# One-query attention over 65,536 keys: second K tile in halves, K1 transposes ahead of the V weights, a tail of 24 slots, and unused matmuls

## The chip, the cores and the metric

The kernel runs on one core of one Trainium2 chip. The metric is the device time of one execution in microseconds (us); lower is better. Each execution is given a state, fast or slow, by its time and the clock that it was granted. PE is the matrix engine (TensorE), PEld its weight loads, DVE the vector engine, ACT the scalar engine, SP the engine that issues nearly all loads.

## The reference

```python
B, Hq, Hkv, Sq, Sk, D = 1, 32, 8, 1, 65536, 128      # bf16
k = jnp.repeat(k, 4, axis=1); v = jnp.repeat(v, 4, axis=1)
scores = jnp.einsum("bhqd,bhkd->bhqk", q, k) * D ** -0.5
return jnp.einsum("bhqk,bhkd->bhqd", _softmax(scores), v)
```

There is one query for each of 32 heads, and 8 groups of keys and values. K and V together are 268.44 MB and are used once. The output is tiny.

## The kernel before

K and V of one group g are cut into two tiles each, K(g,0), K(g,1), V(g,0), V(g,1): 128 partitions x 256 rows x 128 values of bf16, 8.39 MB. The kernel keeps three tiles on chip: one slot for V, one for K(.,0), one for K(.,1). Each load waits until the tile that held its slot has been used.

The loads, in the order in which SP issues them (all code in this section is shortened, with comments added). `s_sc` counts groups of score matmuls; `s_vc` counts half V tiles that PE has finished, two for a tile.

```python
def load_k(g, b):
    SP.wait((s_sc, 16 * g - 8 + 8 * b if g else 0))       # the K tile before it in this slot is used
    cuts = k_cuts.get((g, b), [0, SL])                    # k_cuts: K(0,0) in halves, K(7,1) in quarters
    ...
def load_v(g, b):
    done = 2 * (2 * g + b)
    if (g, b) == (G - 1, 1):                              # the last V tile: a half when half the slot is free, then CUTS
        ...
    elif (g, b) in ((G - 2, 1), (G - 1, 0)):              # V(6,1), V(7,0): in halves, as the slot comes free
        for i in range(2):
            SP.wait((s_vc, done - 1 + i))
            load(v, g, b, 0, s_v[i], 128 * i, 128 * i + 128)
    ...
    else:
        SP.wait((s_vc, done))                             # the whole V tile before it is used
        load(v, g, b, 0, s_v[0])
load_k(0, 0); load_k(0, 1)
for g in range(1, G):
    for b in range(2):
        load_k(g, b); load_v(g - 1, b)
load_v(G - 1, 0); load_v(G - 1, 1)
```

DVE transposes each K tile in four parts in place. It also transposes the softmax weights of a V tile into `et`, which PE needs for that V tile:

```python
for g in range(G):
    for _ in transposes(g, 0): pass                       # 4 x 128x4096
    if g:
        DV.wait((s_vc, 4 * g - 2))                        # PE has finished V(g-1,0): et may be overwritten
        weights(g - 1, 1)
    for i, _ in enumerate(transposes(g, 1)):
        if i == 1: bank_max(g, 0); bank_max(g, 1)
    bank_max(g, 2); ...; softmax(g); ...; weights(g, 0); ...
```

PE runs one loop: scores of K(h,j), then the V tile two behind. Matmuls on V are 64 a tile, each covering 4 row slots; the last `TAIL` slots of the last tile are multiplied one by one in another accumulator after the loop, so that DVE can gather the large accumulator meanwhile:

```python
for ch in range(4):                       # quarters of the V tile
    ...                                   # waits for the loads
    for tt in range(16 if ch < 3 else 12): i = wide(ch, tt)
    if ch == 1: i.then_inc(s_vc, 1)       # half of the V slot is free
```

## Time and profile before

The kernel before takes 636.14 us (median of 4 runs, 635.71 to 636.58).

| | before |
|---|---|
| span of the profile | 634.2 us |
| load queue q1: busy share of 16 DMA engines | 98.4% |
| busy share of PE, DVE | 55%, 55% |
| queue dry near 100 us / near 587 us | 1.50 / 1.93 us |
| end of last load packet to end of span | 5.49 us |

These are lines of the page of the kernel before: the DMA engines' busy tenths and GB/s in 40 slices of the span, the load queue (packets, MB, share), and two DVE groups (busy time, mean ns | idle time before them, and what ended it).

```profile
DMA  8999999999999999999999999999999999999896
GB/s 364 455 438 434 426 397 397 446 413 459 401 459 401 463 401 459 438 422 455 405 459 401 459 403 459 434 422 459 405 455 409 455 409 451 406 438 417 372 429 262
...
q1 hardware_dynamic: 6200, 268.44, 98.4%
...
L237 DVE STREAM_TRANSPOSE io<-io 128x4096 uint32<-128x4096 uint32 x64 | 279.5, 4414 | 92.2 <-DMA io<-in_k_dram 92.2
...
L281 DVE STREAM_TRANSPOSE et<-ex 128x512 bf16<-128x512 bf16 x32 | 21.0, 691 | 97.8 <-PE vacc L359 95.9
```

Loads are busy almost throughout, so only a moment in which the queue is dry, and the time after the last byte, can be saved. Two slices stand out: the 372 GB/s slice near the end, and the last one. DVE waits 97.8 us in all just before it transposes weights, almost all of it for PE's V matmuls; yet most of that waiting costs nothing.

The packet records behind the page give each load packet's start and duration. At each moment one can count how many of the 16 engines have a packet in flight, n, and add up (16-n)/16: that is the "dry" time above. In the steady stretch the last byte of a tile comes 19.34 us after that of the one before: 8.39 MB / 19.34 us = 434 GB/s. The Trainium skill ("DMA: Bandwidth & Descriptors", Specifications) gives 435 GB/s as the ceiling of the fabric, and this trace agrees.

The first hole is seen from the load issues (timeline of SP: start, duration, engine, line, op):

```profile
67.25 0.33 SPq L125 DMA_DIRECT2D io<-in_k_dram  x1
100.68 0.33 SPq L125 DMA_DIRECT2D io<-in_v_dram  x1
```

The issue at 67.25 is K(1,1). The issue at 100.68 is V(0,1). It waits for PE to finish V(0,0). By then the tile issued before it, K(1,1), has landed, so nothing is left in the queue. The second hole is seen in the windows view (window, length, busy time and count of PE, PEld, DVE, ACT, POOL, then granted PE clock, DMA share, GB/s; a packet is booked where it starts), and its cause in the timeline of the last group:

```profile
core 0: us, PE busy (x) PEld busy (x) DVE busy (x) ACT busy (x) POOL busy (x), PEclk, DMA share, GB/s
584.00:586.00 2.00, 2.00 (x16) 0.85 (x19) 0.25 (x1) 0.00 (x0) 0.00 (x0) 1.00 1.07 459
586.00:588.00 2.00, 1.60 (x32) 0.54 (x23) 0.59 (x2) 0.00 (x0) 0.00 (x0) 1.00 0.19 82
588.00:590.00 2.00, 0.91 (x20) 0.50 (x24) 0.00 (x0) 0.00 (x0) 0.00 (x0) 1.00 0.86 262
```

```profile
559.45 1.30 DVE L281 STREAM_TRANSPOSE et<-ex 128x512 bf16<-128x512 bf16 x2 [11.32 <-PE vacc L359]
560.68 8.73 DVE L237 STREAM_TRANSPOSE io<-io 128x4096 uint32<-128x4096 uint32 x2
...
570.51 8.75 DVE L237 STREAM_TRANSPOSE io<-io 128x4096 uint32<-128x4096 uint32 x2
...
585.70 1.90 PE L359 MATMUL vacc<-io,et 128*16 128x512 bf16 x32
...
587.64 27.70 SPq L125 DMA_DIRECT2D io<-in_v_dram  x8
```

Between 586 and 588 us only 82 GB/s start. DVE sat idle for 11.32 us until PE had finished V(6,0), only then transposed the weights and then the four parts of K(7,1), whose first two parts had landed by then (this tile lands between 549.5 and 569.1 us). PE did K(7,1) before V(6,1), so it got to the middle of V(6,1) at 587.6, and V(7,0) could be issued only at 587.64.

The end of the kernel before: 16 single slots (L425), the gather (L355), the scaling (L307); the store follows.

```profile
629.03 1.87 PE L425 MATMUL pf<-io,et 128*4 128x128 bf16 x16 [0.47 <-issue]
...
630.70 0.63 PE L355 MATMUL pf<-vs,sel 128*4 128x128 f32 x2
631.43 0.34 DVE L307 TENSOR_SCALAR o<-pf,rl 4x128 bf16<-4x128 f32 x1 [1.30 <-PE pf L355]
```

### The profile page before, as it was taken

The numbers are of one execution on the slowest core, as the hardware profiler recorded it, in microseconds if no ns is written. First come the engines' busy times: TensorE is split into PE (matmuls) and PEld (weight loads), VectorE is DVE, ScalarE is ACT, GpSimd is POOL, SyncE is SP. The second block draws the span as 40 slices with busy tenths as digits, with TensorE's granted clock in tenths as the row PEclk, the third lists the DMA queues.
The fourth block names the chain that finished last, engine by engine and source line by source line (L and its number), as shares of the span: only waits on it lengthen the run. The fifth ranks groups of instructions, "written<-read, shape, count | busy, mean of one in ns | idle before, by whom it ended". The sixth has DMA issues, their size and how long they took to land. (4 is left out here: it accounts for less than half of the span.)

```text
span 634.2 us, 7031 instructions
## 1 busy us (share of the span) xinstructions
PE 349.6 (55%) x2122; PEld 139.5 (22%) x2122; DVE 347.5 (55%) x239; ACT 36.7 (6%) x72; POOL 7.3 (1%) x39
## 2 busy tenths in 40 slices
PE   0738385836628365382744818447183572858425
PEld 0213132312203122130311303113031230323102
DVE  4938666639156490654807457084660936576201
ACT  0000200020000200002000020000200002000100
POOL 1000000000000000000000000000000000000000
PEclk9978798966959779596896968969587695979755
DMA  8999999999999999999999999999999999999896
GB/s 364 455 438 434 426 397 397 446 413 459 401 459 401 463 401 459 438 422 455 405 459 401 459 403 459 434 422 459 405 455 409 455 409 451 406 438 417 372 429 262
DMA packets 6309, 268.50 MB, mean 423 GB/s; under 512 B 800, under 2 KB 800, under 8 KB 1184
## 3 DMA queue, kind: packets, MB, share of 16 engines
q1 hardware_dynamic: 6200, 268.44, 98.4%
q10 hardware_dynamic: 104, 0.02, 0.0%
q14 instruction: 4, 0.03, 0.0%
q8 instruction: 1, 0.02, 0.0%
HBM read 268.44 MB, written 0.01 MB: 423 GB/s over the span
## 5 line engine op out<-in xcount | busy, mean ns | idle before, releaser
L383 PE MATMUL sc<-io,wz 128*128 x1024 | 272.0, 417 | 211.8 <-PEq L345 169.1
L237 DVE STREAM_TRANSPOSE io<-io 128x4096 uint32<-128x4096 uint32 x64 | 279.5, 4414 | 92.2 <-DMA io<-in_k_dram 92.2
L383 PEld LDWEIGHTS sc<-io,wz 128*128 x1024 | 105.9, 103 | 374.9 <-issue 296.6
L359 PE MATMUL vacc<-io,et 128*16 128x512 bf16 x1020 | 65.3, 409 | 20.1 <-PEq L345 20.1
L281 DVE STREAM_TRANSPOSE et<-ex 128x512 bf16<-128x512 bf16 x32 | 21.0, 691 | 97.8 <-PE vacc L359 95.9
L262 ACT ACTIVATE ex<-sc,nmb 128x512 bf16<-128x512 f32 x32 | 21.5, 685 | 556.9 <-DVE nmb L259 556.9
L242 DVE TENSOR_REDUCE mx<-sc 128x1 f32<-128x512 f32 x32 | 20.7, 667 | 47.6 <-PE sc L383 47.6
L359 PEld LDWEIGHTS vacc<-io,et 128*16 128x16 bf16 x1020 | 26.6, 93 | 57.8 <-issue 36.7
L355 PE MATMUL pf<-vs,sel 128*4 128x128 f32 x20 | 5.2, 358 | 26.8 <-PEq L345 26.8
L251 DVE TENSOR_REDUCE m<-pt 1x4 f32<-1x128 f32 x8 | 2.2, 279 | 22.5 <-PE pt L413 22.5
L272 ACT ACTIVATE sc<-zero 128x2048 f32<-128x2048 f32 x7 | 13.2, 1880 | 0.3
L224 POOL COPY wz<-qT 32x16 bf16<-32x16 bf16 x32 | 6.1, 190 | 509.8 <-PE sc L383 504.5
L372 PE MATMUL pb<-ls,sel 128*4 128x4 f32 x18 | 1.8, 169 | 15.7 <-PEq L345 15.7
L290 DVE TENSOR_SCALAR vs<-vacc,sely 128x128 f32<-128x128 f32 x8 | 2.6, 323 | 14.0 <-PE vacc L359 14.0
L293 DVE SCALAR_TENSOR_TENSOR vs<-vacc,sely,vs 128x128 f32<-128x128 f32 x24 | 8.4, 350 | 0.8
L355 PEld LDWEIGHTS pf<-vs,sel 128*4 128x4 f32 x20 | 1.3, 87 | 27.2 <-issue 27.2
L262 ACT ACTIVATION_READ_ACCUMULATOR ex<-sc,nmb 128x1 f32 x32 | 6.5, 202 | 0.0
L415 PE MATMUL pb<-one,nrow 1*128 1x1 f32 x16 | 2.8, 241 | 5.7 <-PEq L345 5.7
L372 PEld LDWEIGHTS pb<-ls,sel 128*4 128x4 f32 x18 | 1.2, 88 | 18.9 <-issue 18.7
L300 DVE MEMSET vacc<- 128x512 f32 x7 | 3.4, 485 | 1.3 <-DVE vs L293 1.3
L415 PEld LDWEIGHTS pb<-one,nrow 1*128 1x128 f32 x16 | 2.3, 183 | 7.0 <-issue 7.0
L259 DVE COPY nmb<-pb 128x1 f32<-128x1 f32 x8 | 1.3, 157 | 4.3 <-PE pb L415 4.3
(27 smaller groups left out, 21.3 us busy)
## 6 DMA issues: line engine op xcount, KB each, us to landing
io<-in_v_dram SPq DMA_DIRECT2D x5, 4096.0 KB, 18.3
io<-in_k_dram SPq DMA_DIRECT2D x2, 4096.0 KB, 16.6
io<-in_k_dram SPq DMA_DIRECT2D x4, 2048.0 KB, 40.3
io<-in_v_dram SPq DMA_DIRECT2D x1, 2048.0 KB, 10.9
io<-in_v_dram SPq DMA_DIRECT2D x1, 1024.0 KB, 13.0
io<-in_v_dram SPq DMA_DIRECT2D x1, 512.0 KB, 13.9
io<-in_v_dram SPq DMA_DIRECT2D x2, 256.0 KB, 14.1
io<-in_k_dram SPq DMA_DIRECT2D x14, 48.1
```

The lines of the kernel that those rows point to most:

```text
L224: gp.tensor_copy(out=wz[r, :, c0:c0 + H].rearrange("p (s w) h -> p s w h", s=2), in_=qTb[r, :, :, g, :],).then_inc(s_w, 1)
L237: dve.transpose(out=part.bitcast(u32), in_=part.bitcast(u32)).then_inc(s_kt, 2)
L242: return DV.mark(dve.tensor_reduce(out=mx[:, b:b + 1], in_=sc[:, 512 * b:512 * b + 512], axis=AX.X, op=ALU.max))
L262: a = act.activation(out=ex[:, b, :], in_=sc[:, 512 * b:512 * b + 512], func=ACT.Exp, bias=nmb[:, :], scale=SCALE, accum_out=ls[:, b:b + 1],)
L272: ACTQ.mark(act.activation(out=sc[:, :], in_=zero[:, 0:1].to_broadcast([P, 4 * 512]), func=ACT.Copy))
L281: dve.transpose(out=et[:, i, :], in_=ex[:, 2 * b + i, :]).then_inc(s_et, 1)
L293: i = dve.scalar_tensor_tensor(out=vs[:, :], in0=vacc[:, y, :], scalar=sely[:, y:y + 1], in1=vs[:, :], op0=ALU.mult, op1=ALU.add,)
L300: n = DV.mark(dve.memset(vacc[:, :, :], 0.0))
L355: return pe.matmul(out=fin, lhsT=sel[:, :], rhs=vs[:, :], skip_group_check=True, **kw)
L359: return pe.matmul(out=vacc[32 * c:32 * c + 16, :, :], lhsT=et[:, ch // 2, w0:w0 + 16], rhs=io[:, PS * ch + 4 * tt:PS * ch + 4 * tt + 4, : ...
L383: i = pe.matmul(out=bass.AP(sc, r_o, [[2048, P], [1, 512]]), lhsT=bass.AP(wz, r_w + ((2 * s + e) * WB - 4 * u), [[4 * WB, P], [1, P]]), rh ...
L415: pe.matmul(out=pb[:, 0:1], lhsT=nrow[:, :, :].rearrange("o x h -> o (x h)"), rhs=one[:, :], start=True, stop=True,).then_inc(s_pe, 1)
```

## The change

The intent: let the second K tile be transposed as it arrives, let DVE use its wait before the V weights for half of K1, end the large V accumulator sooner (24 single slots for 16, with finer last cuts), and keep the matrix engine's clock up with unused matmuls in each V tile's middle.

```diff
-TAIL = 16
-CUTS = [0, 128, 192, 224, 240, 248, 256]
+TAIL = 24
+CUTS = [0, 128, 192, 224, 232, 240, 248, 256]
...
-    k_cuts = {(0, 0): [0, 128, 256], (G - 1, 1): [0, 64, 128, 192, 256]}
+    k_cuts = {(0, 0): [0, 128, 256], (0, 1): [0, 128, 256], (G - 1, 1): [0, 64, 128, 192, 256]}
...
-        if g:
-            DV.wait((s_vc, 4 * g - 2))
-            weights(g - 1, 1)
         for i, _ in enumerate(transposes(g, 1)):
             if i == 1:
+                if g:
+                    DV.wait((s_vc, 4 * g - 2))
+                    weights(g - 1, 1)
                 bank_max(g, 0)
                 bank_max(g, 1)
...
                     if ch == 1:
                         i.then_inc(s_vc, 1)
+                        for _ in range(3):
+                            pe.matmul(
+                                out=pt[0:16, :], lhsT=et[:, 0, 0:16], rhs=et[:, 0, :],
+                                start=True, stop=True,
+                            )
...      (the tail's loop bounds and waits follow from TAIL and CUTS)
```

More of the change, by code (lines that the diff above doesn't have):

```diff
@@ L399 @@
                         take(s_v[max(ch - 1, 0)], 16)
-                    for tt in range(16 if ch < 3 else 12):
+                    for tt in range(16 if ch < 3 else (SL - TAIL) % PS // 4):
                         if (ch, tt) == (3, 8):
@@ L405 @@
                         i.then_inc(s_vc, 1)
+                        for _ in range(3):
[3 more added lines that the diff above has]
+                            )
                 i.then_inc(s_vb, 1)
                 with pe.If(h * 2 + j < 2 * G + 1):
-                    for tt in range(12, 16):
+                    for tt in range((SL - TAIL) % PS // 4, 16):
                         i = wide(3, tt)
@@ L422 @@
         if x % 8 == 0:
-            pe.wait_ge(s_v[len(CUTS) - 3 + x // 8], 16)
-        w0 = (12 + x // 4) * 32 + 16 + 4 * (x % 4)
+            pe.wait_ge(s_v[4 + x // 8], 16)
+        w0 = t % PS // 4 * 32 + 16 + 4 * (x % 4)
         pe.matmul(
```

## The prediction

> **What bounds the kernel.** The load queue. The page's DMA table gives it 98.4% of the 16 engines' span, 268.44 MB at 423 GB/s; PE and DVE are busy 55% each. In the DMA packet records the 32 K/V tiles land 19.34 us apart in the steady stretch. The Trainium skill ("DMA: Bandwidth & Descriptors", Specifications) gives a ceiling of 435 GB/s; the trace agrees (434). So only dry time of the queue and the work after the last byte can be saved.
>
> **Where it is dry** (packet records over 16 engines: 3.3 us in all):
> - About 100-102 us, 1.5 us. Load V(0,1) waits for the last matmul of V(0,0); it is issued at 100.68, when K(1,1) has just landed. The first packets after it take 3.3 instead of 2.42 us, and this tile lands 22.3 us after the one before: about 2.5-2.9 us lost.
> - About 586.5-589 us, 1.9 us (window 586-588: 82 GB/s). The first half of V(7,0) waits for the middle of V(6,1), which PE reaches at 585.7 because it does K(7,1) first; that waited for DVE, which sat 11.3 us (timeline) behind the weights of V(6,1) while K(7,1) was landing. About 2-2.5 us lost with the restart.
>
> **The change, costed.**
> 1. K(0,1) in halves: DVE waited 10.6 us for the whole tile until 42.1. With a half at about 32.5 PE bounds (8 groups at 2.5 us): K(0,1) ends near 58 instead of 66 us, softmax(0) 8 us sooner, V(0,0) done at about 93-95 instead of 100.7. Hole 1 closes. Cost: 32 KB packets run at 425.5 against 431.6 GB/s, +0.28 us for the tile.
> 2. Half of K1 before the V weights: two 4.40 us transposes move into DVE's idle time; the weights come about 4 us later, off the path. K(7,1) ends on PE at about 581 instead of 585.7, V(7,0) is issued near 583, before the queue is dry at 586.5. Hole 2 closes, with only some 2 us to spare. Steady groups have 8-10 us of queue slack: nothing.
> 3. Tail 24: at the half clock (0.5 from 594 to 631) one single V slot takes 0.117 us. vacc and collect end about 1 us sooner, but PE, with three groups of 8 at 0.94 us, ends near 630.9 as before. About 0.
> 4. Unused matmuls: 3 x 0.43 us cold or 0.22 warm, 16 tiles, all in slack. The skill ("TensorE: Matmul & The Clock Gate", Part 1) says a busy window of about 3.4 us releases the clock; a cold half tile is 3.59 us and becomes 4.9, so the clock may be full at the end. Then the last group of 8 is 0.5 us shorter. Chance even: -0.3 us.
>
> **Sum.** -2.6 - 2.3 + 0.3 - 0.3 = -4.9; rounded for holes that don't close fully: 636.56 to 632.0 us (-0.7%). Range 630.3 to 634.0. Faster by over 2%: 0.01; within: 0.98; slower: 0.01.
>
> **What would show it.** Tiles land 19.4 us apart near 101 and near 588; V(0,1) issued at 92-96 us; no 11 us DVE idle before the V weights in the last group; PE's K(7,1) ends by 582; queue share over 98.8%. Steady groups: same 38.7 us period. The clock in the last 10 us tells of step 4.
>
> **What would make it wrong.** Hole 2 closing only half (2 us of slack); engines drifting apart, so that a removed hole returns as an uneven finish; the unused matmuls delaying the V half; a cold 24-slot tail costing 0.3-0.5 us.

## The result, and the profile after

The changed kernel takes 631.3 us (median of 4 runs, 630.88 to 632.21) against 636.14. The ratio is 0.9926, 95% interval 0.9909 to 0.9943. A ratio here is of the fast runs of both kernels; it is not quite the ratio of the medians quoted, and in the later jobs not exactly that of the means of all runs either. Ten more runs of the unedited kernel in two later jobs gave medians of 631.89 and 632.24, so the first median is on the lucky side (the second job ran on another chip than the third); by the medians of the three jobs the changed kernel is 3.8 to 4.8 us faster than the one before.

The same lines of the page after:

```profile
DMA  8999999999999999999999999999999999999996
GB/s 367 433 459 408 458 408 455 412 454 412 454 412 454 417 450 417 450 417 450 421 446 421 446 425 442 425 442 425 446 425 442 429 437 429 409 433 431 431 428 247
...
q1 hardware_dynamic: 6488, 268.44, 98.9%
...
L237 DVE STREAM_TRANSPOSE io<-io 128x4096 uint32<-128x4096 uint32 x64 | 279.8, 4417 | 162.8 <-DMA io<-in_k_dram 162.8
...
L281 DVE STREAM_TRANSPOSE et<-ex 128x512 bf16<-128x512 bf16 x32 | 20.6, 683 | 15.4 <-PE vacc L359 13.5
```

The queue's share is 98.9%, the slice at 372 GB/s is gone, and DVE now waits 15.4 instead of 97.8 us before weights; it waits for loads instead (162.8 us). Both holes are closed: V(0,1) is issued at 93.86 us, and the windows of the second hole are full.

```profile
59.85 0.33 SPq L125 DMA_DIRECT2D io<-in_k_dram  x1
93.86 0.33 SPq L125 DMA_DIRECT2D io<-in_v_dram  x1
```

```profile
584.00:586.00 2.00, 0.00 (x0) 0.00 (x0) 0.00 (x0) 0.00 (x0) 0.00 (x0) 0.72 0.95 410
586.00:588.00 2.00, 1.67 (x17) 0.60 (x21) 0.00 (x0) 0.00 (x0) 0.00 (x0) 0.50 0.95 410
588.00:590.00 2.00, 2.00 (x21) 0.53 (x13) 0.00 (x0) 0.00 (x0) 0.00 (x0) 0.50 1.14 492
```

The last group after: the first two parts of K(7,1) are transposed as they land, the weights follow without idle time before them, and PE begins V(6,1) at 578.65 instead of 585.70.

```profile
552.17 4.45 DVE L237 STREAM_TRANSPOSE io<-io 128x4096 uint32<-128x4096 uint32 x1 [6.83 <-DMA io<-in_k_dram]
...
557.08 4.45 DVE L237 STREAM_TRANSPOSE io<-io 128x4096 uint32<-128x4096 uint32 x1 [0.47 <-DMA io<-in_k_dram]
...
561.45 1.26 DVE L281 STREAM_TRANSPOSE et<-ex 128x512 bf16<-128x512 bf16 x2
...
563.81 8.75 DVE L237 STREAM_TRANSPOSE io<-io 128x4096 uint32<-128x4096 uint32 x2
...
578.65 1.90 PE L359 MATMUL vacc<-io,et 128*16 128x512 bf16 x32
```

At the end the clock was granted in full in this profile, and 24 slots took less time than 16 before:

```profile
618.87 0.89 PE L408 MATMUL pt<-et 128*16 128x512 bf16 x3
...
624.66 1.50 PE L431 MATMUL pf<-io,et 128*4 128x128 bf16 x24 [0.65 <-DMA io<-in_v_dram]
...
626.00 0.38 PE L355 MATMUL pf<-vs,sel 128*4 128x128 f32 x2
626.48 0.34 DVE L307 TENSOR_SCALAR o<-pf,rl 4x128 bf16<-4x128 f32 x1 [0.91 <-PE pf L355]
```

But the last load packet ends only 3.88 us sooner (624.87 against 628.75), although 3.4 us of dry time and the slow restarts after it are gone. The windows view of the last microseconds of loading shows where some of it went. Before, the loads run at nearly the full rate until the last packet ends at 628.75:

```profile
624.00:626.00 2.00, 1.88 (x16) 0.45 (x16) 0.00 (x0) 0.00 (x0) 0.00 (x0) 0.50 0.97 406
626.00:628.00 2.00, 1.07 (x12) 0.21 (x12) 0.00 (x0) 0.00 (x0) 0.00 (x0) 0.50 1.01 387
```

After, the rate falls off more than 2 us before the last packet ends at 624.87:

```profile
620.00:622.00 2.00, 1.04 (x16) 0.35 (x16) 0.00 (x0) 0.00 (x0) 0.00 (x0) 1.00 1.00 382
622.00:624.00 2.00, 0.98 (x10) 0.26 (x10) 0.00 (x0) 0.00 (x0) 0.00 (x0) 1.00 0.58 216
```

In the last 6 us before the last packet's end, the engines were idle for 0.30 us before and 1.62 us after (packet records). So the mean engine finished 628.75-0.30 = 628.45 us before and 624.87-1.62 = 623.25 us after, 5.2 us sooner, and the slowest one only 3.9 us. About 1.3 us of the gain came back as an uneven finish.

### The profile page after: what moved, and what is told of

It is laid out like the page before. It is cut to its first block, busy times and chain, and to the rows that moved or that the text cites. A ratio compares the mean times of both kernels' runs of the same rounds, so it can differ in the third digit from the quotient of the medians.

```text
span 629.3 us, 7142 instructions
## 1 busy us (share of the span) xinstructions
PE 355.6 (57%) x2176; PEld 141.5 (22%) x2176; DVE 347.1 (55%) x239; ACT 36.7 (6%) x72; POOL 7.4 (1%) x39
## 3 DMA queue, kind: packets, MB, share of 16 engines
q1 hardware_dynamic: 6488, 268.44, 98.9%
## 5 line engine op out<-in xcount | busy, mean ns | idle before, releaser
L383 PE MATMUL sc<-io,wz 128*128 x1024 | 267.3, 411 | 201.5 <-PEq L345 158.4
L237 DVE STREAM_TRANSPOSE io<-io 128x4096 uint32<-128x4096 uint32 x64 | 279.8, 4417 | 162.8 <-DMA io<-in_k_dram 162.8
L359 PE MATMUL vacc<-io,et 128*16 128x512 bf16 x1018 | 73.5, 409 | 19.8 <-PEq L345 19.7
L281 DVE STREAM_TRANSPOSE et<-ex 128x512 bf16<-128x512 bf16 x32 | 20.6, 683 | 15.4 <-PE vacc L359 13.5
L408 PE MATMUL pt<-et 128*16 128x512 bf16 x48 | 13.7, 397 | 0.0
L408 PEld LDWEIGHTS pt<-et 128*16 128x16 bf16 x48 | 4.6, 95 | 6.6 <-issue 1.6
```

The source lines that it names most:

```text
L237: dve.transpose(out=part.bitcast(u32), in_=part.bitcast(u32)).then_inc(s_kt, 2)
L281: dve.transpose(out=et[:, i, :], in_=ex[:, 2 * b + i, :]).then_inc(s_et, 1)
L359: return pe.matmul(out=vacc[32 * c:32 * c + 16, :, :], lhsT=et[:, ch // 2, w0:w0 + 16], rhs=io[:, PS * ch + 4 * tt:PS * ch + 4 * tt + 4, : ...
L383: i = pe.matmul(out=bass.AP(sc, r_o, [[2048, P], [1, 512]]), lhsT=bass.AP(wz, r_w + ((2 * s + e) * WB - 4 * u), [[4 * WB, P], [1, P]]), rh ...
L408: pe.matmul(out=pt[0:16, :], lhsT=et[:, 0, 0:16], rhs=et[:, 0, :], start=True, stop=True,)
```

## The experiments

Theory: the gain is the two holes, less what an uneven finish gives back, and the clock at the end adds a little by chance. Rivals: the gain is the clock in the tail; the uneven finish comes from the small last pieces; the unused matmuls merely delay. All times are medians of 5 runs; gains are differences of means. The kernel before took 636.12, 636.19 and 636.04 us (medians of 9 runs) in the three jobs. All twelve runs gave correct results. The time in the table is the median; the other columns come from one profiled run, which need not be a typical one: it was the fastest of its five for dve_order (634.01 us), unused_only (636.33) and no_unused_2 (632.19), and the slowest for both_holes (633.31), after_again (633.07), after_third (632.53) and unused_8 (632.04).

| run | time | dry near 100 / 587 us | idle in last 6 us of loading | after last packet |
|---|---|---|---|---|
| before (its own profile) | 636.1 | 1.50 / 1.93 | 0.30 | 5.49 |
| k01_halves | 633.71 | 0.02 / 1.92 | 0.29 | 5.47 |
| dve_order | 635.32 | 1.22 / 0.01 | 1.47 | 4.65 |
| both_holes | 632.24 | 0.02 / 0.04 | 2.06 | 5.50 |
| no_unused | 632.71 | 0.00 / 0.01 | 1.33 | 5.13 |
| no_unused_2 | 632.67 | 0.00 / 0.01 | 1.58 | 5.06 |
| changed (its own profile) | 631.3 | 0.00 / 0.00 | 1.62 | 4.44 |
| after_again | 631.89 | 0.00 / 0.01 | 1.69 | 5.77 |
| after_third | 632.24 | 0.00 / 0.00 | 1.73 | 5.77 |
| tail16 | 631.84 | 0.00 / 0.01 | 1.76 | 5.54 |
| unused_8 | 631.07 | 0.00 / 0.00 | 1.17 | 5.37 |
| warm_end | 631.89 | 0.01 / 0.01 | 1.64 | 4.80 |
| hole_put_back | 637.82 | 0.00 / 7.09 | 0.23 | 5.02 |
| unused_only | 638.14 | 2.57 / 2.56 | 0.19 | 4.56 |

### k01_halves: one load change alone, on the kernel before

```diff
-    k_cuts = {(0, 0): [0, 128, 256], (G - 1, 1): ...
+    k_cuts = {(0, 0): [0, 128, 256], (0, 1): [0, 128, 256], (G - 1, 1): ...
```

> The kernel before with only the second K tile in halves. Theory (two dry holes of the load queue): V(0,1) is issued near 94 us as in the changed kernel, the hole at 100 us is gone, the hole near 587 us stays at about 1.9 us; 2.5 us off, about 633.6 us. Because the late hole lets all engines finish together again, the last packets of the 16 engines end within 0.6 us of each other. Rival (the gain comes from the clock in the tail): no gain, 636 us.

Measured 633.71 us, ratio 0.996 (0.9947 to 0.9974), 2.50 us by the means. The load V(0,1) is issued at 92.91 us:

```profile
92.91 0.33 SPq L125 DMA_DIRECT2D io<-in_v_dram  x1
```

The first hole is gone, the second as it was, and the engines finish together. All as expected; the tail-clock rival falls, since the time after the last packet did not change (5.47 us).

### dve_order: the other load change alone, on the kernel before

```diff
-        if g:
-            DV.wait((s_vc, 4 * g - 2))
-            weights(g - 1, 1)
         for i, _ in enumerate(transposes(g, 1)):
             if i == 1:
+                if g:
+                    DV.wait((s_vc, 4 * g - 2))
+                    weights(g - 1, 1)
                 bank_max(g, 0)
                 bank_max(g, 1)
```

> The kernel before with only half of each K1 tile transposed ahead of the V weights. Theory: the hole at 100 us stays (1.5 us of idle queue), the hole near 587 us is gone; about 2 us off, 634 us; the last packets end 1 us or more apart, since nothing after 100 us lets the engines meet again. Rival (tail clock): no gain, 636 us.

Measured 635.32 us, ratio 0.9987 (0.9973 to 1.0), 1.08 us by the means: half of what was expected, and only just clear of the noise (the interval reaches 1.0). The mechanism works (timeline: the weights come without a wait, V(6,1) begins at 581.47, the second hole is 0.01 us):

```profile
559.83 4.45 DVE L237 STREAM_TRANSPOSE io<-io 128x4096 uint32<-128x4096 uint32 x1 [0.46 <-DMA io<-in_k_dram]
...
564.20 1.26 DVE L281 STREAM_TRANSPOSE et<-ex 128x512 bf16<-128x512 bf16 x2
...
581.47 1.90 PE L359 MATMUL vacc<-io,et 128*16 128x512 bf16 x32
```

But the idle time of the last 6 us rises from 0.30 to 1.47 us. Closing 1.92 us of hole gave 1.17 us of uneven finish. The loads of this profile end 1.18 us sooner than before (627.57 against 628.75), which fits the 1.08; that its time is as low as 634.01 us comes from a tail of 4.65 us, with the clock full from 626.6 to 633.4 us.

### both_holes: the two load changes together, on the kernel before

> The kernel before with both load changes, the tail of 16 slots and no unused matmuls. Theory: both holes gone, the last packet ends near 625 us as in the changed kernel, and the work after it takes the 5.4 us of the kernel before, not 4.4: about 632.2 us. Rival (tail clock): 636 us.

Measured 632.24 us, ratio 0.9938 (0.9924 to 0.9952), 3.71 us by the means. The single gains were 2.50 and 1.08, sum 3.58. By the means the whole change gained 4.72, 4.24 and 4.11 us in its three jobs, so these two edits carry most of the result, and they do it with 5.50 us after the last packet, as before. The rest isn't shown to belong to any one edit.

### no_unused and no_unused_2: the changed kernel without the unused matmuls

```diff
-                        for _ in range(3):
-                            pe.matmul(out=pt[0:16, :], ...)
```

> The changed kernel without the unused matmuls, with its tail of 24 slots. Theory: clock 0.5 through the last V tile, the 24 single slots take 2.8 instead of 1.5 us, the work after the last packet some 1 us longer: about 632.3 us, 0.7 to 1.2 us over the changed kernel. Rival (the unused matmuls only delay): the same as the changed kernel or faster, 631 us.

> The changed kernel without the unused matmuls once more, now in the same rounds as the changed kernel. Theory: 0.3 to 0.6 us slower than it, about 632.3 us. Rival (3 of them do nothing that the scatter of the runs would show): within 0.2 us.

> The changed kernel unedited, for the comparison with the two runs before it: 631.8 us; idle of 1.2 to 2 us in the last 10 us of loading; the clock at the end differs from the two profiles taken so far, since the windows fall as they fall.

The first gave 632.71 us, ratio 0.994 (0.9927 to 0.9954). The second gave 632.67 us beside 632.24 us for the changed kernel of the same rounds; the means are 632.54 and 631.87, which would make 3 unused matmuls worth 0.67 us. But the intervals of the two ratios (0.9934 to 0.9961 and 0.992 to 0.9947) overlap, and the single runs do too (632.19 to 632.93 and 631.07 to 632.53), so even the sign isn't shown. Nor do the profiles show where such a gain would arise: the time after the last packet was 5.13 and 5.06 us without these matmuls, against 4.44, 5.77 and 5.77 us in the three profiles with them. The expectation of an extra microsecond in the tail was missed.

### after_again and tail16: the changed kernel unedited, and with the old tail

```diff
-TAIL = 24
-CUTS = [0, 128, 192, 224, 232, 240, 248, 256]
+TAIL = 16
+CUTS = [0, 128, 192, 224, 240, 248, 256]
```

> The changed kernel once more, unedited, as the measure of the runs beside it and to see whether the uneven finish repeats: 631.3 us; engine idle time of 1.2 to 2 us (sum over 16 engines, divided by 16) in the last 10 us of loading, none near 100 and 587 us.

> The changed kernel with the old tail of 16 single slots and the old cuts. Theory as predicted (24 slots worth about 0): the same as the changed kernel within 0.3 us. Rival (24 slots end the V accumulator sooner, and that is on the path when the clock is full): 0.5 to 1 us slower.

Medians 631.89 and 631.84, means 631.98 and 631.76. The 24 slots are worth nothing measurable. The uneven finish repeats in all three profiles of the changed kernel: 1.62, 1.69, 1.73 us. The full clock at the end does not repeat. In after_again (timeline), the 24 slots took 2.72 us, and in after_third 2.72 us too, against 1.50 us in the first profile:

```profile
619.51 1.48 PE L408 MATMUL pt<-et 128*16 128x512 bf16 x3
...
625.22 2.72 PE L431 MATMUL pf<-io,et 128*4 128x128 bf16 x24 [0.65 <-DMA io<-in_v_dram]
```

The clock record explains it. In after_again the clock was full from 621.7 to 625.1 and half from 625.1 to 628.5, just when the slots ran. In one of three profiles the full clock reached the end: that was luck.

### unused_8 and warm_end: more unused matmuls

```diff
-                        for _ in range(3):
+                        for _ in range(8):          # unused_8
```

```diff
                     if ch == 1: ...
+                        unused(6)                   # warm_end: for the 3
+                    if ch == 2: unused(3)
                     ...
                         if (ch, tt) == (3, 8):
+                            unused(1)
                     ...
+    unused(2)
     for x in range(TAIL):
```

> The changed kernel with 8 unused matmuls a V tile for 3. Theory (they release the clock for the end, and 3 do so only in some phases): clock 1.0 from about 620 us to the end in the profile, work after the last packet 4.4 us or less, 630.9 us, 0.2 to 0.5 us under the changed kernel. Rival (they delay the V slot): loads of V up to 1 us later, no hole, the same or slower.

> The changed kernel with its unused matmuls spread over the pauses of each V tile: 6 in the middle, 3 before the third quarter's end, 1 before the last cut, 2 before the single slots. Theory (the clock at the end is a matter of how busy each 3.4 us window is): clock 1.0 without a break from about 618 us to the end, the work after the last packet 4.4 us in the profile, 630.9 us, 0.5 to 1 us under the changed kernel of the same rounds, and closer runs. Rival (the clock at the end is chance, or the matmuls delay the slots): the same 631.8 us, or slower.

unused_8 gave 631.07 us (ratio 0.9921, 0.9907 to 0.9934) beside 631.89 for after_again (0.9915 to 0.9942): 0.6 us better by the means, but the intervals overlap, so it stays unclear whether it beats the changed kernel. Its profile missed the expectation: the clock was full from 618.4 to 625.2 and half afterwards. That run was the slowest of its five and was granted 0.831 of the clock on average, the other four 0.843, so those may have come closer to what was expected. warm_end did what was expected of the clock: full from 620.2 to 630.5 us, and its 24 slots took 1.50 us.

```profile
624.82 0.59 PE L368 MATMUL pt<-et 128*16 128x512 bf16 x2 [0.65 <-issue]
...
625.25 1.50 PE L438 MATMUL pf<-io,et 128*4 128x128 bf16 x24
```

Yet its time, 631.89 us, is no better than that of the changed kernel of the same rounds (means 631.89 and 631.87); its runs only lie closer (631.57 to 632.30 against 631.07 to 632.53). In the lines above the slots begin at 625.25, 0.17 us after the last packet's end at 625.08; in after_third they began at 624.67, before the last packet's end at 624.97. It may be that the two unused matmuls ahead of them hold them up; no run takes them away. I found no version that clearly beats the changed kernel.

### hole_put_back: the second hole reopened

```diff
             for i in range(2):
-                SP.wait((s_vc, done - 1 + i))
+                SP.wait((s_vc, done if g == G - 1 else done - 1 + i))
```

> The changed kernel, but the first half of V(7,0) waits for the end of V(6,1) and not for its middle, so that the queue runs dry for about 5 us near 586 us. Theory (a dry hole lets the 16 engines meet again, so closing one gives part of it back as an uneven finish): idle of 5 us in the hole, but only 0.2 to 0.4 us in the last 10 us of loading instead of 1.5, so the time rises by 1 to 1.5 us less than the hole: about 635.2 us. Rival (the uneven finish comes from the small last pieces): 1.5 us idle at the end still, 636.5 us.

Measured 637.82 us, ratio 1.0019 (1.0005 to 1.0033). The windows show a longer hole than I expected, because V(7,0) now waits for the second half of V(6,1) to land and to be multiplied:

```profile
584.00:586.00 2.00, 0.00 (x0) 0.00 (x0) 0.00 (x0) 0.00 (x0) 0.00 (x0) 0.50 0.08 33
586.00:588.00 2.00, 1.63 (x16) 0.61 (x20) 0.00 (x0) 0.00 (x0) 0.00 (x0) 0.50 0.00 0
588.00:590.00 2.00, 2.00 (x21) 0.55 (x13) 0.00 (x0) 0.00 (x0) 0.00 (x0) 0.50 0.00 0
```

The test is in the sum. 7.09 us of hole were put in, and by the means (637.52 - 631.98) the time rose by 5.54 us. The idle time in the last 6 us fell from 1.69 to 0.23 us, and 7.09 - (1.69 - 0.23) = 5.63; the last packet of the two profiles ends 5.50 us apart (631.01 and 625.51). The last pieces were not changed, so the rival (small pieces make the finish uneven) falls. A dry queue lets the engines meet again; without one, what separates them stays to the end. (What separates them is read from the packet records, at the end of the next section.) The table says the same of all fourteen profiles: four with a hole near 587 us have 0.19 to 0.30 us of idle finish, ten without one have 1.17 to 2.06.

### unused_only: the unused matmuls alone, on the kernel before

> The kernel before with the unused matmuls alone. Theory: both holes stay, so 0 to 0.5 us off, 635.9 us; V(0,1) issued up to 0.7 us later (3 matmuls at the full clock in V(0,0)), so the first hole may even grow by that: then 636.3 us. Rival (the gain of the change is the clock): 634 us or less.

Measured 638.14 us, ratio 1.0032 (1.0018 to 1.0045): 1.67 us slower by the means. Both holes grew, from 1.50 and 1.93 to 2.57 and 2.56 us, 1.70 us together. (The profile is that of the fastest of the five runs, 636.33 us: its loads end 1.23 us later than before, its tail is 0.93 us shorter. No profile of the slower runs was kept.) The unused matmuls stand before the end of the V tile, for which the next V load waits:

```profile
98.82 0.38 PE L408 MATMUL pt<-et 128*16 128x512 bf16 x1
...
99.26 2.10 PE L359 MATMUL vacc<-io,et 128*16 128x512 bf16 x26
101.41 0.33 SPq L125 DMA_DIRECT2D io<-in_v_dram  x1
```

V(0,1) is issued at 101.41 instead of 100.68 us. I had expected the direction but too small a size (636.3 us). So these matmuls cost time while the holes exist, and become harmless only when the other two edits have closed them. The clock rival falls here for good.

## Why the prediction was right

The time on record, 632.0 us, holds: 631.3 in the first job, 631.9 and 632.2 in the later ones, all within 630.3 to 634.0 and within 2%. By parts:

- **What bounds the kernel: right.** Only dry time and the end could be saved, and the queue share rose to 98.9%. The tiles of the steady stretch land 19.35 us apart, as before (19.34).
- **Hole 1 (-2.6 + 0.3 us): right.** k01_halves measured -2.50 us. K(1,1) was issued at 59.85 instead of 67.25, V(0,1) at 93.86, inside the 92 to 96 that was written. The cost of smaller packets, 0.3 us, was over-stated: two 32 KB packets take 2 x 1.213 us against 2.418 for one of 64 KB, which is 0.06 us a tile (128 partitions / 16 engines x 0.008).
- **Hole 2 (-2.3 us): right mechanism, wrong size.** V(7,0) was issued at 580.59, even sooner than "near 583", and the hole closed completely, so the fear of only 2 us of slack was needless. But dve_order measured -1.08 us. The difference is the uneven finish, which the text named as a danger ("a removed hole returns as an uneven finish") but did not subtract: +1.2 us there, +1.3 us in the changed kernel.
- **Tail of 24 (0): right.** tail16 differs by 0.2 us in the means, in favour of 16, which is within the scatter.
- **Unused matmuls (-0.3 us): not shown.** In the changed kernel they measured -0.67 us, within the scatter of the runs; one of three profiles had the full clock in the tail. The statement "all in slack" is true only after the two holes are closed: alone they cost 1.67 us.

The mechanism of both holes was right, but that the total came so close is partly luck: hole 2 was put 1.2 us too high, and this was offset by the rounding from 4.9 to about 4.6, by the over-stated cost of small packets and by what the unused matmuls may have given.

Why some engines come late can be read from the packet records. They carry no engine number, but in a busy queue nearly every load packet begins within 0.05 us of the end of another one, so the records of a profile fall into 16 chains, taken here as one for each engine (in the changed kernel each moves 16.7 to 16.8 MB, a sixteenth of the load). Between 10 and 610 us each profile has five packets of the kind "instruction" (four of 8 KB taking about 0.3 us, one of 16 KB taking about 1 us). In the first profile of the changed kernel they begin at 41.64, 106.92, 375.40, 417.52 and 561.59 us, and each time one chain pauses until the instruction packet ends, and its next load packet is 0.38 to 0.66 us slower than usual: 0.7 to 1.6 us lost on that engine. At the first of them a second chain pauses too, for 0.95 us, which I can't explain. Between 45 and 612 us nothing else holds up a chain by more than 0.13 us. So the engines do not drift: they fall behind in steps, one engine at a time, and at 583 us the last chain is 2.7 us of work behind the first, with the same distance at 610 us. All fourteen profiles show a pause at each of their five instruction packets (both_holes also has slow load packets near 593 us that this doesn't explain). The second hole of the kernel before shows how they meet: the chains are idle there for 0.09 to 2.81 us, and all begin again between 588.60 and 589.24 us. This is read from traces; no run moves the instruction packets.

## What to carry to other kernels

In a kernel bound by its loads, look for the moments in which the load queue runs dry, and follow each back to the slot that came free too late; that is where edits on other engines can pay. Expect somewhat less than the length of the hole, because a dry queue also lets the parallel load engines catch up with each other, and what they no longer lose there shows up as an uneven finish. An edit that fills idle time on another engine must be tested together with the edits that make that time idle: here unused matmuls cost 1.7 us alone and nothing measurable beside the others.

## What the Trainium skill lacked or had wrong

- "DMA: Bandwidth & Descriptors" remarks in passing, in a note on another kind of traffic that it marks as unconfirmed, that a bulk load runs at the pace of its slowest engine. It does not say that an engine which falls behind in an unbroken queue stays behind until the queue runs dry: 1.17 to 2.06 us of idle finish without a late hole, 0.19 to 0.30 us with one.
- No page says how long an instruction packet holds up the load engine that carries it: 0.7 to 1.6 us at each of the five in the first profile of the changed kernel.
- The Specifications of "DMA: Bandwidth & Descriptors" list about 358 GB/s as the limit of HBM for one core, without the condition that the same page gives further down (Bandwidth, Measured): both cores that share the memory loading at once. With one core working, the page of the profile shows 423 GB/s before and 427 GB/s after over the whole span.
- The same page gives a fixed cost for a DMA issued from GpSimd, but not that the first packets after a dry queue are slow themselves: at the first hole 64 KB packets took about 3.0 to 3.4 us against 2.42 us in the steady stretch.
- "TensorE: Matmul & The Clock Gate", Part 1, says the clock drops after at least one idle window of about 3.4 us. In after_again the stretch from 621.7 to 625.1 us was not idle (PE was busy on V for 1.66 of its 3.40 us), and the next 3.4 us were at half clock all the same. How busy a window must be is not stated; no run here settles it.
